# Output stores on ScalarE's queue, spread q loads and fewer w_out transfers in a fused linear-attention and mish kernel

## The chip, the cores and the metric

The kernel runs on one core of one Trainium2 chip. The time is device microseconds from one execution to its end, the median of three runs. PE is the matmul engine, PEld its weight loads, DVE VectorE, ACT ScalarE, POOL GpSimd; SP only issues transfers. DMA engines move data between HBM and the on-chip memory, and a transfer is issued by an instruction on the queue of SP or ACT.

## The reference

```python
kv  = einsum('bhsd,bhse->bhde', k, v)          # 8 x 8 heads, 576 tokens, 64 wide
out = einsum('bhsd,bhde->bhse', q, kv)
out = out / sqrt(mean(out * out, -1) + 1e-6) * g_norm
x   = out.transpose(0, 2, 1, 3).reshape(4608, 512)
h   = x @ w_in                                 # 512 x 2048
g   = h * tanh(softplus(h))                    # mish
return g @ w_out                               # 2048 x 512
```

All in float32; w_in and w_out arrive as float64 and are read as pairs of 32-bit words.

## The kernel before, in words

The work has two parts. The first computes x and g = mish(x @ w_in) and writes g to scratch memory in HBM (`gd`, nine tiles of 512 tokens); the second reads g back and multiplies by w_out.

Both products are done by a Winograd form of Strassen's scheme: seven products of half-size blocks instead of eight. Left forms (A11, S1, ...) come from the activations, right forms (B11, T1, ...) from the weights. Each form is split by `split` (L118 to L120) into a rounded part (an ACT cast) and a rest (a DVE subtraction), and each product takes three matmuls per slice.

Part one has nine blocks i of 512 tokens, each with four groups n (`NQ`), each group with seven steps, one for each product: 252 steps in all. A step is one of p0 to p6 in `group`. PE multiplies into two PSUM tiles `a` and two `bc`; ACT copies out of them (L372 to `ul`, L377 and L386 to `ur`), DVE adds (L427), ACT applies mish (L116), and the two finished tiles `ul` and `ur`, 512 KB each, are stored to `gd` (L425, L432). There are two rooms each for `ul` and `ur`: the copy of two groups later must wait for the store.

Beside the products of block i the attention of block i + 1 goes on: `kv_load` (L204, L205) and `kv_product` (L240) for k and v, a unit of two pairs of heads at a time for q (`load` L272, DVE transpose L285, projection L297 to L302, square L306, sums L317 to L320, Ln and Exp L325 and L326, normalize L330), and the left forms of the next x. ACT loads another function table when it changes between mish and Ln or Exp (L116, L324). Also beside it, w_out is read (L134, sixteen tiles of four source pieces), scaled and joined from its words (L139 to L146), made into forms (`wst`) and stored to scratch memory `wod` (L191). In the last block the forms of w_out come back (L550) into the rooms of w_in's forms, and g begins to be read (L555).

The order: `at(t, f)` puts a piece of work at step t of the plan, and the instructions are written in the plan's order. The compiler's scheduler orders PE, DVE, ACT and GpSimd itself; SP's queue stays as written (`manual_schedule` for SP), so SP issues each transfer only after those written ahead of it. All transfers, of either queue, share eight semaphores in turn, and a transfer waits for the last one on its semaphore to land.

Of the kernel before, what the change touches and what calls it, by code (L numbers as in the profile page):

```python
# [7 lines left out]
F32 = mybir.dt.float32  # L8
# [12 lines left out]

A11, S1, S2, S4, A12, S3, A22 = range(7)

T1, T3, T2, T4, B11, B22, B21 = range(7)

PROD = ((A11, B11, "a"), (S1, T1, "c"), (A22, T4, "p"), (S2, T2, "a"), (S4, B22, "c"), (A12, B21, "b"), (S3, T3, "a"))

# [2 lines left out]
def linear_attention_rms_mish_ffn(  # L30
# [95 lines left out]
    def weight_forms(srcs, m, n, forms, put=None):  # L126

        st = {}
        w = m * n

        def load():
            t = wpools["w64"].tile([P, 4, w, 2], U32, name="w64")
            for i, src in enumerate(srcs):
                nc.sync.dma_start(t[:, i].rearrange("p (m n) t -> p m (n t)", m=m), src)  # L134
            st["w"] = t.rearrange("p b n t -> p (b n) t")

        def scale():
            st["x"] = wpools["wx"].tile([P, 4 * w], F32, name="wx")
            nc.scalar.mul(st["x"], st["w"][:, :, 1].bitcast(F32), 2.0 ** -112)  # L139

        def join():
            low, high = st["w"][:, :, 0], st["w"][:, :, 1]
            t = st["x"].bitcast(U32)
            nc.vector.tensor_single_scalar(t, t, 3, ALU.logical_shift_left)
            nc.vector.scalar_tensor_tensor(t, high, 0x80000000, t, ALU.bitwise_and, ALU.bitwise_or)
            nc.vector.scalar_tensor_tensor(t, low, 29, t, ALU.logical_shift_right, ALU.bitwise_or)  # L146

        def differences():
            x = st["x"].rearrange("p (b n) -> p b n", b=4)
            d = st["w"].rearrange("p n t -> p (n t)").bitcast(F32)[:, 0:4 * w].rearrange("p (b n) -> p b n", b=4)  # L150
            nc.vector.tensor_sub(d[:, 0:2], x[:, 1:3], x[:, 0:2])
            nc.vector.tensor_sub(d[:, 2], x[:, 2], d[:, 0])
            nc.vector.tensor_sub(d[:, 3], x[:, 3], d[:, 2])
            st["x"], st["d"] = x, d
            st["f"] = forms()

        def parts(f0, f1, src):
            hi, lo = (st["f"][:, f0:f1, s].rearrange("p f m n -> p f (m n)") for s in range(2))
            split(hi, lo, src)

        def first():
            parts(T1, T4 + 1, st["d"])

        def rest():
            parts(B11, B11 + 1, st["x"][:, 0:1])
            parts(B22, B21 + 1, st["x"][:, 2:4])

        def store():
            put(st["f"])

        return load, scale, join, differences, first, rest, store
# [3 lines left out]
    def weight_in(j):  # L175
        def forms():
            wf[j] = wfp.tile([P, 7, 2, 2, P], F32R, name="wf")
            return wf[j]
        srcs = []
        for kh, r in ((0, 0), (0, 1), (1, 1), (1, 0)):  # L180
            c0 = 2 * P * (j + r * NF2)
            src = w_in[kh * 2 * P:(kh + 1) * 2 * P, c0:c0 + 2 * P]
            srcs.append(src.rearrange("(m p) n -> p m n", p=P))
        return weight_forms(srcs, 2, P, forms)

    def weight_out(c, h):
        def forms():
            return wpools["wst"].tile([P, 7, 2, 1, P], F32R, name="wst")

        def store(f):  # L190
            nc.sync.dma_start(wod[c][:, :, :, h * P:(h + 1) * P], f.rearrange("p f s m n -> p f s (m n)").bitcast(F32))  # L191
        srcs = []
# [27 lines left out]
    def kv_new(b):  # L220
        def new(name, dtype):
            t = kvs.tile([P, NKC, P], dtype, name=name)
            nc.vector.memset(t.bitcast(F32), 0.0)
# [28 lines left out]
    def segments(j):  # L252

        n = (S - T) * j
        segs = []
        if n:
            segs.append((j - 1, S - n, slice(0, n)))
        if n < T:
            segs.append((j, 0, slice(n, T)))
        return segs  # L260

    def unit_steps(j, u):
        st = {}

        def load(n):
            if n == 0:
                st["q"] = att.tile([P, 2, T], F32, name="qs")
            for i in range(2 * n % 4, 2 * n % 4 + 2):
                a, h, d0 = n // 2, 4 * u + 2 * (n // 2) + i // 2, 32 * (i % 2)
                for b, s0, cols in segments(j):  # L270
                    n_ = cols.stop - cols.start
                    nc.sync.dma_start(  # L272
                        st["q"][32 * i:32 * i + 32, a, cols].rearrange("p (c d) -> p c d", d=32),
                        q[b, h, s0:s0 + n_, d0:d0 + 32].rearrange("(c p) d -> p c d", p=32),
                    )

        def parts(t):
            hi = att.tile([P, 2, T], F32R, name="fh")
# [142 lines left out]
    def put_in(st, block, bank):  # L421
        o, i, n, t = u_dst(st, block), st["i"], st["n"], 7 * (NQ * st["i"] + st["n"])
        if block == "21":
            mish(o, bank)
            at(t + 11, lambda: nc.sync.dma_start(gd[i][:, 2 * n:2 * n + 2, :], st["ul"]))  # L425
            return
        nc.vector.tensor_add(o, bank, o)  # L427
        if block == "11":
            mish(o, o)
        elif block == "22":  # L430
            mish(st["ur"], st["ur"])
            at(t + 9, lambda: nc.sync.dma_start(gd[i][:, NF2 + 2 * n:NF2 + 2 * n + 2, :], st["ur"]))  # L432


    NS = 7 * NQ
# [8 lines left out]
    nc.vector.memset(eps, 1e-6)  # L444
    nc.vector.memset(ones.bitcast(F32), 0.0)
    nc.vector.memset(ones[0:D, 0:D].bitcast(F32), 1.0)
    nc.vector.memset(ones[D:P, D:P].bitcast(F32), 1.0)
# [5 lines left out]
    for step in START.split():  # L453
        what, n = step[0], int(step[1:])
        load, transpose, project, square, sums, rstd, normalize = units[0][n % 2]
        if what == "w":
            conv[n] = weight_in(n)
            conv[n][0]()
        elif what == "c":
            for f in conv[n][1:6]:  # L460
                f()
        elif what == "k":
            ts = []
            for m in range(2):
                ts.append(rooms[2 * n + m])
                ts.append(x[0:SL, 2 * n + m, 0:4 * D].rearrange("p (h d) -> p h d", h=4))
            kv_tiles[n] = kv_load(0, 4 * n, 4, ts)
        elif what == "m":
            kv_product(0, 4 * n, 4, *kv_tiles[n])
        elif what == "q":  # L470
            for i in range(4):
                load(i)
        elif what == "t":
            transpose()
            project()
        elif what == "s":
            square()
            sums()
        elif what == "r":
            rstd()  # L480
            normalize()
        elif what == "a":
            x_sums(n)
        elif what == "f":
            x_form(n)
# [10 lines left out]
    def attention(j):  # L496

        t = NS * (j - 1)
        if j < B:
            st = {}  # L500

            def kload(p):
                st[p] = kv_load(j, 2 * p, 2, kv_staging())

            def kmul(p):
                kv_product(j, 2 * p, 2, *st[p])
            at(t, lambda: kv_new(j))
            for p in range(4):
                at(t + 3 * p - 2 if p else max(t - 18, -1), lambda p=p: kload(p))
                at(t + 3 * p, lambda p=p: kmul(p))  # L510
        for u, ns in enumerate(((3, 5, 6, 8, 9, 10), (12, 14, 15, 17, 18, 19))):
            for s, n in enumerate(ns):
                at(t + n, units[j][u][s + 1])
            for n in range(4):
                at(t + 4 + n if u else max(t - 14 + n, -1), lambda u=u, n=n: units[j][u][0](n))
        at(t + 20, lambda: x_sums(0))
        for f, n in zip(range(7), (21, 22, 24, 25, 26, 27, 30)):
            at(t + n, lambda f=f: x_form(f))
            if f == S1:
                at(t + n, lambda: x_sums(1))  # L520
# [228 lines left out]
```

## Time and profile before

| | |
|---|---|
| time, median of three runs | 927.61 us (926.47 to 931.49) |
| profiled execution | 924.8 us, its span 923.0 us |
| mean granted clock of PE | 0.974 |
| busy: PE, DVE, ACT, POOL | 841.3, 597.7, 512.5, 0.2 us |
| moved by DMA | 160.50 MB, 174 GB/s over the span |

A busy PE is not a PE at its peak. Issues of transfers, register and semaphore instructions are not counted as busy. In the chain that ended last, "SPq" is time in SP's queue, "DMA" a transfer in flight, "issue" time without a cause in the profile. A line such as "PE a L409 <- ACT ul L116: 13.2, 5, 3.9" says who waited (engine, tile, line), for whom, how many us in all, how often, and the longest.

### The profile page before, as it was taken

The page shows a single profiled execution, that of the slowest core. Times are in us where ns is not written, and L with a number is a line of the kernel's source. Part 1 is how long each engine was busy: PE and PEld are TensorE (multiplying, and loading weights), DVE is VectorE, ACT ScalarE, POOL GpSimd, SP SyncE. Part 2 cuts the span into 40 slices and gives each one's busy share as a digit, 9 for nine tenths or more (in the row PEclk, how much of TensorE's full clock was granted, in tenths as well). Part 3 has the DMA queues.
Part 4 walks back from the last instruction along what each step waited for, and adds up shares of the span by engine and source line. Part 5 has one row for each costly group of instructions (what it writes and reads, how often), then busy time and mean ns, then how long its engine had stood idle before and what let it go on. Part 6 is the DMA issues. An engine that isn't in the chain of part 4 may idle for free.

```text
span 923.0 us, 17036 instructions
## 1 busy us (share of the span) xinstructions
PE 841.3 (91%) x6940; PEld 809.6 (88%) x6940; DVE 597.7 (65%) x842; ACT 512.5 (56%) x776; POOL 0.2 (0%) x4
## 2 busy tenths in 40 slices
PE   3498799897989889989899998999999999999997
PEld 1286699797988879989898998899999999999997
DVE  4688874836557465575755526867776677776661
ACT  2577666776567676677776534444444444444441
POOL 0000000000000000000000000000000000000000
PEclk9789899999999999999999999999999999999999
DMA  8557547766674776667463999433334433333411
GB/s 188 164 143 228 173 116 208 239 171 190 172 206 158 206 218 190 183 202 205 156 191 118 348 391 353 163 119 133 114 120 162 153 115 124 128 116 124 161 59 46
DMA packets 204973, 160.50 MB, mean 174 GB/s; under 512 B 91744, under 2 KB 190048, under 8 KB 203872
## 3 DMA queue, kind: packets, MB, share of 16 engines
q1 hardware_dynamic: 204896, 159.42, 56.1%
q8 instruction: 54, 0.88, 0.4%
q14 instruction: 23, 0.19, 0.1%
HBM read 97.52 MB, written 61.87 MB: 173 GB/s over the span
## 4 chain that ended last, share of the span: by engine, by line
PE 61%; SPq 13%; DMA 11%; ACT 10%; DVE 3%; issue 2%; ACTq 0%; DVEq 0%
PE a L598 21%; PE bc L598 16%; PE a L409 12%; SPq L272 8%; PE bc L409 7%; DMA wf<-wod 3%; SPq L134 3%; DMA gd<-ur 2%; DMA gd<-ul 1%; PE s L240 1%; PE q L666 1%; DMA w<-in_moe_w_out_dram 1%; ACT ur L116 1%; DMA w<-in_moe_w_in_dram 1%; ACT ul L116 1%
## 5 line engine op out<-in xcount | busy, mean ns | idle before, releaser
L409 PE MATMUL a<-gf,wf 128*128 128x256 f32 x1728 | 242.9, 293 | 34.0 <-ACT ul L116 13.2
L409 PEld LDWEIGHTS a<-gf,wf 128*128 128x128 f32 x1728 | 225.8, 198 | 43.5 <-ACT ul L116 14.3
L598 PE MATMUL a<-wf,gf 128*128 128x256 f32 x1632 | 203.4, 284 | 2.8 <-ACT ul L372 2.3
L598 PEld LDWEIGHTS a<-wf,gf 128*128 128x128 f32 x1632 | 199.6, 190 | 3.2 <-ACT ul L372 2.5
L409 PE MATMUL bc<-gf,wf 128*128 128x256 f32 x1296 | 180.2, 288 | 5.7 <-DVE wf L120 3.0
L409 PEld LDWEIGHTS bc<-gf,wf 128*128 128x128 f32 x1296 | 167.6, 195 | 8.8 <-DVE wf L120 3.5
L598 PE MATMUL bc<-wf,gf 128*128 128x256 f32 x1224 | 153.1, 284 | 0.2 <-DVE gf L120 0.2
L120 DVE TENSOR_TENSOR gf<-g,gf 128x1024 fp32r<-128x1024 f32 (+1 forms) x100 | 109.7, 1103 | 63.0 <-ACT gf L119 63.0
L598 PEld LDWEIGHTS bc<-wf,gf 128*128 128x128 f32 x1224 | 149.7, 189 | 0.4 <-DVE gf L120 0.4
L119 ACT CAST gf<-g 128x1024 fp32r<-128x1024 f32 (+1 forms) x100 | 94.5, 954 | 59.5 <-PE bc L598 55.2
L119 ACT CAST gf<-s 128x1024 fp32r<-128x1024 f32 (+2 forms) x58 | 49.2, 850 | 36.1 <-PE a L598 29.3
L120 DVE TENSOR_TENSOR gf<-s,gf 128x1024 fp32r<-128x1024 f32 (+2 forms) x58 | 56.3, 972 | 12.1 <-ACT gf L119 12.0
L372 ACT COPY ul<-a 128x512 f32<-128x512 f32 (+1 forms) x53 | 27.3, 516 | 47.6 <-PE a L598 29.3
L120 DVE TENSOR_TENSOR fl<-fa,fh 128x1024 fp32r<-128x1024 f32 x28 | 34.2, 1221 | 19.8 <-ACT fh L119 19.6
L427 DVE TENSOR_TENSOR ul<-bc,ul 128x512 f32<-128x512 f32 x36 | 24.8, 689 | 33.6 <-ACT ul L372 27.7
L116 ACT ACTIVATE ur<-ur 128x1024 f32<-128x1024 f32 x36 | 38.0, 1055 | 15.4 <-DVE ur L427 15.2
L427 DVE TENSOR_TENSOR ur<-bc,ur 128x512 f32<-128x512 f32 x36 | 24.8, 689 | 28.7 <-ACT ur L386 12.4
L120 DVE TENSOR_TENSOR gf<-gf 128x512 fp32r<-128x512 f32 x45 | 30.4, 685 | 13.6 <-ACT gf L119 12.0
L427 DVE TENSOR_TENSOR ur<-a,ur 128x512 f32<-128x512 f32 x36 | 24.7, 687 | 15.7 <-PE a L409 15.6
L116 ACT ACTIVATE ul<-a 128x512 f32<-128x512 f32 x36 | 21.4, 594 | 22.2 <-PE a L409 22.0
L330 DVE SCALAR_TENSOR_TENSOR gf<-x,gcol,fa 128x1024 f32<-128x1024 f32 x18 | 23.1, 1282 | 16.4 <-ACT fa L326 16.3
L139 ACT ACTIVATE wx<-w 128x512 f32<-128x512 f32 (+1 forms) x24 | 20.0, 833 | 23.4 <-DMA w<-in_moe_w_out_dram 13.3
(95 smaller groups left out, 843.0 us busy)
## 6 DMA issues: line engine op xcount, KB each, us to landing
g<-gd SPq DMA_DIRECT2D x18, 2048.0 KB, 8.7
gd<-ur SPq DMA_DIRECT2D x36, 512.0 KB, 3.1
gd<-ul SPq DMA_DIRECT2D x36, 512.0 KB, 3.8
wod<-wst SPq DMA_DIRECT2D x16, 896.0 KB, 5.3
wf<-wod SPq DMA_DIRECT2D x8, 1792.0 KB, 13.5
out_dram<-ul SPq DMA_DIRECT2D x18, 512.0 KB, 2.8
w<-in_moe_w_in_dram SPq DMA_DIRECT2D x32, 256.0 KB, 3.9
w<-in_moe_w_out_dram SPq DMA_DIRECT2D x64, 128.0 KB, 3.1
```

What stands on the lines that cost most here:

```text
L116: in_turn(nc.scalar.activation(o, i, AF.Mish))
L119: nc.scalar.copy(hi, src)
L120: nc.vector.tensor_sub(lo, src, hi.bitcast(F32))
L134: nc.sync.dma_start(t[:, i].rearrange("p (m n) t -> p m (n t)", m=m), src)
L139: nc.scalar.mul(st["x"], st["w"][:, :, 1].bitcast(F32), 2.0 ** -112)
L240: nc.tensor.matmul(ps[o * D:(o + 1) * D, i, :], kt, vt, start=(c == 0), stop=(c == CM))
L272: nc.sync.dma_start(st["q"][32 * i:32 * i + 32, a, cols].rearrange("p (c d) -> p c d", d=32), q[b, h, s0:s0 + n_, d0:d0 + 32].rearrange("( ...
L330: nc.vector.scalar_tensor_tensor(o, st["x"], gcol, st["r"], ALU.mult, ALU.mult)
L372: nc.scalar.copy(dst(st, "11"), st["a"])
L409: nc.tensor.matmul(bank[:, jj], w[:, right, a, kc, :], xf[:, b, kc, :], start=first and jj == kc == s == 0, stop=(kc == 1 and s == 2), ski ...
L427: nc.vector.tensor_add(o, bank, o)
L598: nc.tensor.matmul(bank, gf[:, a, c, :], wo[c][:, right, b, :], start=first and c == s == 0, stop=(c == NF2 - 1 and s == 2), skip_group_ch ...
```

## The change

Stores of `ul` and `ur` are issued by ACT, planned at t + 10 and t + 7 instead of t + 11 and t + 9. q is loaded in eight pieces of one 32-row part each instead of four of two parts, at steps t - 15, t - 13, ..., t - 1 for the first unit (before: t - 14 to t - 11) and t + 4 to t + 11 for the second (before: t + 4 to t + 7); its transposes stay at t + 3 and t + 12. A w_out tile is read by two transfers of 256 KB instead of four of 128 KB; for that the forms B22 and B21 change places. Ten memsets move from DVE to GpSimd.

```diff
-T1, T3, T2, T4, B11, B22, B21 = range(7)
+T1, T3, T2, T4, B11, B21, B22 = range(7)
...
         def load():
             t = wpools["w64"].tile([P, 4, w, 2], U32, name="w64")
+            n_ = 4 // len(srcs)
             for i, src in enumerate(srcs):
-                nc.sync.dma_start(t[:, i].rearrange("p (m n) t -> p m (n t)", m=m), src)
+                dst = t[:, i].rearrange("p (m n) t -> p m (n t)", m=m) if n_ == 1 else t[:, n_ * i:n_ * i + n_].rearrange("p b n t -> p b (n t)")
+                nc.sync.dma_start(dst, src)
...
-            nc.vector.tensor_sub(d[:, 0:2], x[:, 1:3], x[:, 0:2])
-            nc.vector.tensor_sub(d[:, 2], x[:, 2], d[:, 0])
-            nc.vector.tensor_sub(d[:, 3], x[:, 3], d[:, 2])
+            nc.vector.tensor_sub(d[:, 0:2], x[:, 1:4:2], x[:, 0:2])
+            nc.vector.tensor_sub(d[:, 2], x[:, 3], d[:, 0])
+            nc.vector.tensor_sub(d[:, 3], x[:, 2], d[:, 2])
...
-        for fh, r in ((0, 0), (0, 1), (1, 1), (1, 0)):
-            f0, c0 = (c + fh * NF2) * P, 2 * (r * DM // 2 + h * P)
-            srcs.append(w_out[f0:f0 + P, c0:c0 + 2 * P].rearrange("p (m n) -> p m n", m=1))
+        for fh in range(2):
+            f0 = (c + fh * NF2) * P
+            srcs.append(w_out[f0:f0 + P, :].rearrange("p (r h n) -> p r h n", r=2, h=2)[:, :, h, :])
...
-            nc.vector.memset(t.bitcast(F32), 0.0)
+            nc.gpsimd.memset(t.bitcast(F32), 0.0)
...
-            for i in range(2 * n % 4, 2 * n % 4 + 2):
-                a, h, d0 = n // 2, 4 * u + 2 * (n // 2) + i // 2, 32 * (i % 2)
+            a, i = divmod(n, 4)
+            h, d0 = 4 * u + 2 * a + i // 2, 32 * (i % 2)
...
-            at(t + 11, lambda: nc.sync.dma_start(gd[i][:, 2 * n:2 * n + 2, :], st["ul"]))
+            at(t + 10, lambda: nc.scalar.dma_start(gd[i][:, 2 * n:2 * n + 2, :], st["ul"]))
...
-            at(t + 9, lambda: nc.sync.dma_start(gd[i][:, NF2 + 2 * n:NF2 + 2 * n + 2, :], st["ur"]))
+            at(t + 7, lambda: nc.scalar.dma_start(gd[i][:, NF2 + 2 * n:NF2 + 2 * n + 2, :], st["ur"]))
...
-            for n in range(4):
-                at(t + 4 + n if u else max(t - 14 + n, -1), lambda u=u, n=n: units[j][u][0](n))
+            for n in range(8):
+                at(t + 4 + n if u else max(t - 15 + 2 * n, n // 2 - 1), lambda u=u, n=n: units[j][u][0](n))
```

SP's queue in the third block of part one (i = 2, `gd_92`), from the w_out words of one tile to those of the next, before:

```order
L134 DMA w_2068<-in_moe_w_out_dram 128x256 x4
L272 DMA qs<-in_q_dram 32x8x32 x4
L191 DMA wod_100<-wst 1792x1x128
L272 DMA qs<-in_q_dram 32x8x32 x8
L432 DMA gd_92<-ur 128x1024
L272 DMA qs<-in_q_dram 32x8x32 x4
L425 DMA gd_92<-ul 128x1024
L432 DMA gd_92<-ur 128x1024
L134 DMA w_2318<-in_moe_w_out_dram 128x256 x4
L425 DMA gd_92<-ul 128x1024
```

The same place in the changed kernel:

```order
L136 DMA w_2060<-in_moe_w_out_dram 128x2x256 x2
L274 DMA qs<-in_q_dram 32x8x32 x2
L193 DMA wod_100<-wst 1792x1x128
L274 DMA qs<-in_q_dram 32x8x32 x10
L136 DMA w_2304<-in_moe_w_out_dram 128x2x256 x2
L274 DMA qs<-in_q_dram 32x8x32 x2
L193 DMA wod_101<-wst 1792x1x128
L274 DMA qs<-in_q_dram 32x8x32 x2
```

The four stores are gone from SP's queue, and four of the sixteen pieces of q stand behind the next w_out words.

ACT's queue around the mish of the second `ur` of that block, before (its store is the first L432 above):

```order
L116 ACT_TABLE_LOAD
L116 ACTIVATE ul<-ul 128x2x256
L248 CAST kvh_350<-s_1978 64x64
L116 ACTIVATE ur<-ur 128x1024
L377 COPY ur<-bc 128x2x256
L119 CAST fh<-fa 128x1024
L248 CAST kvh_350<-s_1978 64x64
L116 ACTIVATE ul<-a 128x2x256
```

In the changed kernel, with the semaphores that each instruction waits for (DMAHW with a number is one of the eight of the transfers):

```order
L116 ACT_TABLE_LOAD
L116 ACTIVATE ul<-ul 128x2x256 [waits DVE_49]
L116 ACTIVATE ur<-ur 128x1024 [waits DVE_49]
L374 COPY ul<-a 128x2x256 [waits DMAHW0_49,PE_49]
L434 DMA gd_92<-ur 128x1024 [waits DMAHW5_49,Activation_49]
L250 CAST kvh_338<-s_1965 64x64 [waits PE_49]
L379 COPY ur<-bc 128x2x256 [waits DMAHW2_49,PE_49]
L250 CAST kvh_338<-s_1965 64x64 [waits DVE_49]
L116 ACTIVATE ul<-a 128x2x256 [waits PE_49]
L326 ACT_TABLE_LOAD
L427 DMA gd_92<-ul 128x1024 [waits DMAHW2_49,Activation_49]
```

Two stores now stand in ACT's order, each one or two instructions behind its mish; besides that mish each waits for a semaphore on which an earlier transfer, here of q on SP's queue, must have landed, and the copy of the next `ur` stands behind the first of them.

More of the change, by code (lines that the diff above doesn't have):

```diff
@@ L165, in rest @@
             parts(B11, B11 + 1, st["x"][:, 0:1])
-            parts(B22, B21 + 1, st["x"][:, 2:4])
+            parts(B21, B22 + 1, st["x"][:, 2:4])
         def store():
@@ L179, in weight_in @@
         srcs = []
-        for kh, r in ((0, 0), (0, 1), (1, 1), (1, 0)):
+        for kh, r in ((0, 0), (0, 1), (1, 0), (1, 1)):
             c0 = 2 * P * (j + r * NF2)
@@ L267, in load @@
                 st["q"] = att.tile([P, 2, T], F32, name="qs")
-            for i in range(2 * n % 4, 2 * n % 4 + 2):
-                a, h, d0 = n // 2, 4 * u + 2 * (n // 2) + i // 2, 32 * (i % 2)
[L270 to L275, printed above, removed]
+            a, i = divmod(n, 4)
+            h, d0 = 4 * u + 2 * a + i // 2, 32 * (i % 2)
+            for b, s0, cols in segments(j):
+                n_ = cols.stop - cols.start
+                nc.sync.dma_start(
+                    st["q"][32 * i:32 * i + 32, a, cols].rearrange("p (c d) -> p c d", d=32),
+                    q[b, h, s0:s0 + n_, d0:d0 + 32].rearrange("(c p) d -> p c d", p=32),
+                )
         def parts(t):
@@ L443, in linear_attention_rms_mish_ffn @@
         nc.sync.dma_start(gcol[r, :], g_norm.rearrange("(p o) -> p o", o=1))
[L444 to L447, printed above, removed]
+    nc.gpsimd.memset(eps, 1e-6)
+    nc.gpsimd.memset(ones.bitcast(F32), 0.0)
+    nc.gpsimd.memset(ones[0:D, 0:D].bitcast(F32), 1.0)
+    nc.gpsimd.memset(ones[D:P, D:P].bitcast(F32), 1.0)
     weight_pools(2, 1, 0)
@@ L470, in linear_attention_rms_mish_ffn @@
         elif what == "q":
-            for i in range(4):
+            for i in range(8):
                 load(i)
```

## The prediction, as it was on record before the run

> **What bounds the kernel now.** I read the page's busy line and its chain that ended last first, then a table of stretches, then the waits inside the stretch that has room, and last one event of the chain in order of time.
>
> ```profile
> PE 841.3 (91%) x6940; PEld 809.6 (88%) x6940; DVE 597.7 (65%) x842; ACT 512.5 (56%) x776; POOL 0.2 (0%) x4
> PE 61%; SPq 13%; DMA 11%; ACT 10%; DVE 3%; issue 2%; ACTq 0%; DVEq 0%
> ```
>
> PE looks full, yet 13% of the chain is SP's queue issuing transfers and 11% is transfers in flight. The stretches (start:end, length, then busy time of PE, weight loads, DVE, ACT, POOL, granted clock, DMA share, GB/s) say where that can be:
>
> ```profile
> 49.00:108.00 59.00, 47.86 (x370) 41.39 (x368) 51.29 (x78) 42.86 (x71) 0.00 (x0) 0.93 0.70 200
> 108.00:508.00 400.00, 368.60 (x3108) 353.48 (x3108) 246.06 (x420) 279.27 (x436) 0.00 (x0) 0.97 0.63 182
> 508.00:579.00 71.00, 65.41 (x533) 63.99 (x531) 36.31 (x74) 32.09 (x63) 0.00 (x0) 1.00 1.00 365
> 579.00:923.00 344.00, 338.95 (x2808) 338.54 (x2808) 235.13 (x231) 137.33 (x182) 0.00 (x0) 0.99 0.36 121
> ```
>
> From 579 us on PE is never short of work (339 of 344 us); the change does not reach there. From 508 to 579 the DMA engines are full (share 1.00) and PE has 5.6 us idle. The room is in the 400 us before: 31.4 us in which PE is idle. What ended that idle time (waiter, its line, released by: total us, times, longest):
>
> ```profile
> PE a L409 <- ACT ul L116: 13.2, 5, 3.9
> PE a L409 <- ACT ul L372: 9.0, 6, 3.8
> PE a L409 <- ACT ur L386: 5.1, 5, 1.9
> PE bc L409 <- ACT ur L377: 2.8, 3, 1.5
> ACT ul L372 <- DMA gd<-ul: 7.3, 7, 2.4
> ACT ur L377 <- DMA gd<-ur: 11.3, 7, 2.9
> ACT wx L139 <- DMA w<-in_moe_w_out_dram: 13.3, 10, 3.7
> SPq L432 <- ACT ur L116: 62.1, 13, 9.7
> SPq L204 <- PE s L240: 36.7, 11, 7.3
> ```
>
> 13.2 + 9.0 + 5.1 + 2.8 = 30.1 us of PE's idle time ends on ACT. ACT is no full engine (279 of 400 us): it waits 18.6 us for stores of earlier outputs, whose room it wants to write, and 13.3 us for words of w_out. Those transfers are late because SP issues everything in one written order: it stands 62.1 us before stores of ur whose mish is not done, and the loads behind stand with it; and a store that is ready stands behind the loads ahead of it. One event of the chain (start, us, what):
>
> ```profile
> 200.85 1.06 ACT ur L116
> ...
> 208.40 1.29 SPq L272
> ...
> 214.32 5.20 DMA gd<-ur
> 219.55 0.59 ACT ur L377
> 220.13 0.96 ACT fa L326
> 221.11 1.28 ACT L116
> 222.41 0.63 ACT ul L116
> 223.03 0.94 ACT ur L116
> 223.98 0.49 ACT ul L116
> 224.52 4.50 PE a L409 x24
> ...
> 358.43 2.92 PE a L409 x24
> 453.76 4.63 PE a L409 x24
> ```
>
> The mish of ur ends at 201.9; its store is issued at 214.3, 12.4 us late, behind eight pieces of q. It lands at 219.5, and only then ACT may copy into that ur again; behind it in ACT's order stand the Exp, a table load and three mishes, and PE waits for the last of them. After such a gap 24 matmuls take 4.50 or 4.63 us instead of 2.92: these two rows make 1.6 + 1.7 = 3.3 us more that belong to the gaps. PE's own timeline of the event, with the idle time before a piece in brackets:
>
> ```profile
> 220.18 1.69 PE L409 MATMUL bc<-gf,wf 128*128 128x256 f32 x12 [1.48 <-ACT ur L377]
> 224.52 4.49 PE L409 MATMUL a<-gf,wf 128*128 128x256 f32 x24 [2.65 <-ACT ul L116]
> ```
>
> **The change part by part.** Prices of an issue and of a landing:
>
> ```profile
> L425 SPq DMA_DIRECT2D gd<-ul x36: 319/389/1698, 84.6 to 562.1; - x36
> L432 SPq DMA_DIRECT2D gd<-ur x36: 319/350/2242, 81.0 to 561.4; - x36
> L272 SPq DMA_DIRECT2D qs<-in_q_dram x256: 311/467/2124, 6.7 to 470.9; - x128
> ...
> DMA to landing us min/median/max: 1.7/2.4/6.7
> ...
> L134 SPq DMA_DIRECT2D w<-in_moe_w_out_dram x64: 423/432/1823, 103.3 to 464.4; - x64
> gd<-ur SPq DMA_DIRECT2D x36, 512.0 KB, 3.1
> gd<-ul SPq DMA_DIRECT2D x36, 512.0 KB, 3.8
> w<-in_moe_w_in_dram SPq DMA_DIRECT2D x32, 256.0 KB, 3.9
> w<-in_moe_w_out_dram SPq DMA_DIRECT2D x64, 128.0 KB, 3.1
> ```
>
> Stores, the gain. Issued by ACT soon after its own mish, a store of ur lands some 3.1 us later and one of ul 3.8 us later, where their rooms are wanted about a group of seven steps later. A group takes (562.1 - 84.6)/35 = 13.6 us by the ul row, so the 18.6 us of ACT's waits for stores should go. SP loses 72 issues and the 62.1 us of standing still, so the w_out words come earlier too: I take half of 13.3, 6.6 us. In the event above ACT's wait is the longest of its kind, 2.9 us, and PE's two gaps behind it are 1.48 + 2.65 = 4.1 us: 2.9/4.1 is 70%. I take 70% of the 30.1 us: **-21.1 us**. Ends: all of it with the slow matmuls, -33.4, or nothing, if what is next in line is just as late (below). What is late next is ACT's own bunch of Exp, table load and mishes, 4.3 us in the rows above.
>
> Stores, the cost. The issue now stands in ACT's own order. No trace here shows an issue by ACT; the nearest rows are SP's issues of the same transfers, median 0.39 and 0.35 us, so 0.37 each (ends: the 0.32 of the smallest and the 2.2 of the longest, which came in the stretch with full DMA engines). 400/13.6 = 29.4 groups make 59 stores in the stretch with room, 59 x 0.37 = 21.8 us. Each waits for the mish that ACT itself has just done, so no other compute engine is waited for. Behind a store stand copies out of PSUM, and PE waits for those. ACT has 10% of the chain, 92 us, nearly all of it before 579 us, which is 16% there; with SP's and DMA's parts gone I let it double, to a third: 21.8 / 3 = **+7.3 us**. Ends: 0 and 21.8.
>
> The Trainium skill (DMA: Bandwidth & Descriptors, Issuing engines are not separate DMA queues) says that transfers issued by different engines run on the same 16 DMA engines and interleave, so that spreading them saves only the issuing engine's time, usually little. By that rule the term above would be +7.3 and the gain nearly none; against it stands the event above, where the loss was 12.4 us of standing in line and not bandwidth, at a DMA share of 0.63.
>
> q in eight pieces: the same 256 issues of 0.47 us. They are spread over fifteen and eight steps instead of four, and for the second unit the last piece stands one step (1.95 us) before its transpose instead of five, with an issue of two parts and a landing ahead of it, 2 x 0.47 and 2.4 us: 1.4 us late, eight times, and more at the longest landing, 6.7; but the steps only set SP's order, SP has nothing to wait for there after its k and v loads, and DVE, which transposes, is busy 246 of 400 us. PE has no wait on the projections in the stretch. I take 0; ends 0 and +10.
>
> w_out by two transfers: 32 fewer issues of 0.43 us, 13.8 us of SP's time, which no longer bounds. Landing: four issues and 3.1 us were 4.8; two issues and the 3.9 of a 256 KB load are 4.8. 0, ends -2 and +2. The order of the blocks inside the forms (B21 before B22) moves no work: one tensor operation reads with a step; 0.
>
> Memsets on GpSimd:
>
> ```profile
> L223 DVE MEMSET kvh<- x3: 485/485/485, 1.1 to 86.0; 128x512 f32 x3
> ```
> ```profile
> 32.34 0.26 ACT kvh L244
> ```
>
> DVE loses ten instructions, six of them of 0.49 us (three of kvh, as many of kvl). Four of the six come from 1.1 us on, before there are data; the last two, at 86 us, stand where DVE is busy 51 of 59 us, so up to -1. GpSimd's price isn't in the trace (its four memsets of one column are 0.2 us together); in the chain the first of these tiles is written by ACT at 32.3 us, so 30 us of loading cover it. 0; ends -1 and +2.
>
> The end of the first part. From 508 us two stores (1 MB, at 365 GB/s 2.9 us) of the last group no longer stand behind the last w_out forms in one queue but run beside them: +1.5, half of it; ends 0 and 2.9.
>
> Sum against the profiled execution's 924.8 us: -21.1 + 7.3 + 1.5 = -12.3, 912.5 us. That execution lies 2.8 below the median of the runs, 927.6; so **915 us**.
>
> **The rivals.**
>
> The bunch on ACT keeps its time. Exp, table load and the three mishes follow each other in any case, so a store that lands in time moves a gap without closing it. For it: 13.2 of the 30.1 us end on a mish and not on a copy. Against it: in the event the wait comes first. With 35% instead of 70%: -10.5 + 7.3 + 1.5 = -1.7, 926 us. The rule of the Trainium skill cited above, that only issue time is saved, would end here too.
>
> SP's queue leaves the chain altogether, and the matmuls after gaps run at full rate. 90% of 33.4 is -30.1; with a sixth of the issues on the path (+3.6) and the +1.5, -25.0: 903 us. For it: SPq is 13% of the chain, 120 us, far more than PE's idle time. Against it: ACT is at 70% and takes 21.8 us more.
>
> Slower: ACT inherits SP's wait. The order of instructions shows that a store on ACT waits for one of eight DMA semaphores that both queues share, so for an earlier load on SP, mostly a piece of q, to land; and SP still stands before its k and v loads until PE has used the last ones, 36.7 us in 11 waits. If ACT stands there with it, all of PSUM's copies stand behind: 0.7 x 36.7 = +25.7, so -12.3 + 25.7 = +13.4, 938 + 2.8 = 941 us. It decides from about 12.3/0.7 = 18 us of such waits on. Against it: the loads in question stand a few places ahead of the store, and SP no longer stands before stores.
>
> **How the numbers follow.** Chances: forecast (906 to 922) 0.59; SP gone from the chain (below 906) 0.10; bunch (923 to 932) 0.17; ACT inherits the wait (above 932) 0.14. The range reaches from the second rival's 903, less 3 for the lower ends of w_out and the memsets, to the edge of the slower case: 900 to 932. About 0.5%, 4.6 us, is what a measurement of this kernel can tell from no change: faster 0.69, same 0.17, slower 0.14.
>
> **What would show it.** Right: ACT's waits for gd in the first 508 us fall from 18.6 to under 5, for w_out words to under 8; stores are issued within 2 us of their mish; SPq falls from 13% of the chain to under 7; PE's idle time that ends on ACT falls to 8 to 15 us; ACT's queue issues 72 transfers of about 0.37 us; GpSimd has ten memsets more and no one waits for them. Wrong: ACT standing before its stores for pieces of q, or PE idle behind Exp and mishes as long as before (then the bunch bounds), or DVE's transposes waiting for the last piece of q and PE for the projections.

## The result and the profile after

The changed kernel is slower: 963.89 us, median of four runs (962.0 to 965.83), against 929.0 us (926.47 to 931.49). The ratio is 1.0376 with an interval of 1.0335 to 1.0417. The prediction said 915 us and 900 to 932. The profiled execution took 965.35 us, its span is 963.6 us and its mean granted clock 0.946 (before 0.974).

The busy line and the chain that ended last, of the page after:

```profile
PE 858.5 (89%) x6940; PEld 823.7 (85%) x6940; DVE 596.3 (62%) x832; ACT 510.3 (53%) x776; POOL 3.6 (0%) x14
PE 44%; DMA 6%; ACT 2%; DVE 1%; issue 1%; SPq 0%; ACTq 0%
```

DVE and ACT are busy no longer than before (ACT's 72 issues are not counted) and POOL has only the ten memsets more; PE's 6940 matmuls, the same as before, now take 17 us longer. The chain adds up to only 54% of the span, since it was not followed back through most of part one. That SPq stands at 0% in it therefore says nothing about the first part. The stretches say where the time is (columns as before):

```profile
49.00:108.00 59.00, 47.87 (x356) 41.91 (x355) 46.48 (x70) 40.08 (x67) 1.06 (x2) 0.86 0.68 183
108.00:544.00 436.00, 384.14 (x3138) 365.51 (x3138) 251.44 (x427) 280.35 (x443) 0.00 (x0) 0.93 0.59 172
544.00:620.00 76.00, 66.03 (x512) 64.67 (x511) 37.42 (x74) 32.28 (x62) 0.00 (x0) 0.94 0.88 336
620.00:963.00 343.00, 338.82 (x2804) 338.42 (x2803) 233.18 (x228) 135.51 (x178) 0.00 (x0) 0.99 0.36 119
```

The last 343 us are those of before. The loss lies ahead of them. Cut at the last matmul of part one, this is the first part before, then after:

```profile
49.00:560.40 511.40, 467.42 (x3896) 445.22 (x3894) 322.01 (x553) 347.41 (x560) 0.00 (x0) 0.97 0.67 203
```
```profile
49.00:598.50 549.50, 482.38 (x3886) 457.25 (x3886) 320.95 (x551) 344.19 (x560) 1.06 (x2) 0.93 0.62 189
```

It is 549.5 - 511.4 = 38.1 us longer. PE's idle time grew from 511.4 - 467.4 = 44.0 us to 549.5 - 482.4 = 67.1, by 23.1. The other 15.0 us are the same matmuls run at a granted clock of 0.93 instead of 0.97. What ended PE's idle time in the 436 us stretch:

```profile
PE a L411 <- ACT ul L116: 18.0, 8, 6.5
PE s L321 <- DVE fl L120: 9.7, 3, 6.0
PE a L411 <- DVE ur L429: 7.3, 4, 3.6
PE a L411 <- ACT ul L374: 4.5, 3, 2.7
PE a L411 <- ACT ur L388: 3.8, 3, 1.4
PE a L411 <- DVE wf L120: 3.2, 1, 3.2
PE bc L411 <- ACT ur L379: 3.0, 2, 2.7
```

The four rows of ACT that the prediction summed to 30.1 us now sum to 18.0 + 4.5 + 3.8 + 3.0 = 29.3: nothing was gained there. New are 9.7 + 7.3 + 3.2 = 20.2 us that end on DVE. What ACT and SP stood for in the same stretch:

```profile
ACT wx L141 <- DMA w<-in_moe_w_out_dram: 29.9, 11, 4.7
ACT fh L119 <- DVE fa L287: 16.6, 5, 5.5
ACT ul L374 <- DMA gd<-ul: 16.2, 11, 3.5
ACT wst L119 <- DMA wod<-wst: 11.1, 7, 3.4
```
```profile
SPq L206 <- PE s L242: 113.5, 18, 16.3
SPq L557 <- DVE gf L332: 21.0, 1, 21.0
SPq L274 <- DMA qs<-in_q_dram: 16.7, 8, 3.5
SPq L274 <- DVE fa L287: 16.1, 6, 9.0
```

ACT's wait for stores of `ur` (11.3 us before) has gone, but that for stores of `ul` has grown from 7.3 to 16.2 us, so of the 18.6 us for both, 16.2 are left. Its wait for words of w_out has grown from 13.3 to 29.9 us, and a wait for the transposes of q is new. SP no longer stands before stores: before, the two largest rows were 62.1 us there and 36.7 us before its k loads, 98.8 together, and now it is 113.5 us before the k loads alone. With the smaller rows of the same lines, SP stood 101.7 us before stores, 44.7 before k and v loads and 1.4 before pieces of q; now it is 128.4 us before k and v loads and 36.5 before pieces of q. The standing moved from one place of the queue to others, and the sum did not get smaller.

One event shows a path from there to PE. These are rows of the timeline of SP, ACT, DVE and PE (start, us, idle time before in brackets):

```profile
146.07 0.38 SPq L206 DMA_DIRECT2D km<-in_k_dram  x1
...
148.49 9.76 SPq L274 DMA_DIRECT2D qs<-in_q_dram  x6
158.29 1.24 SPq L136 DMA_DIRECT2D w<-in_moe_w_out_dram  x2
...
168.44 2.22 SPq L136 DMA_DIRECT2D w<-in_moe_w_out_dram  x2
...
155.19 1.25 DVE L287 STREAM_TRANSPOSE fa<-qs 128x1024 f32<-128x1024 f32 x1 [1.94 <-DMA qs<-in_q_dram]
...
156.48 1.05 ACT L119 CAST fh<-fa 128x1024 fp32r<-128x1024 f32 x1 [5.52 <-DVE fa L287]
162.48 0.67 ACT L141 ACTIVATE wx<-w 128x512 f32<-128x512 f32 x1 [3.46 <-DMA w<-in_moe_w_out_dram]
173.78 0.66 ACT L141 ACTIVATE wx<-w 128x512 f32<-128x512 f32 x1 [4.07 <-DMA w<-in_moe_w_out_dram]
...
178.81 5.49 PE L411 MATMUL a<-gf,wf 128*128 128x256 f32 x24 [6.47 <-ACT ul L116]
```

The k load at 146.07 is the first of the next block, planned at t + 10; SP reaches it when PE has done the product before it. The last of the second unit's eight pieces of q, two transfers, is planned behind it, at t + 11, and goes out from 148.49 on; before the change the last piece was planned at t + 7, ahead of this load. These two transfers took 5.3 and 6.3 us to land, where the median from 146 to 176 us is 2.3. The transpose, which needs all eight pieces, runs at 155.19 (in the profile before, the same one runs at 145.50), and ACT stands 5.5 us for it. There is one room for `qs`, so the next unit's pieces wait for this transpose, and the w_out words that are written behind them go out at 158.29. ACT stands 3.46 us for these words, and 4.07 us for those of the next tile, which go out from 168.44 on. The Exp, a table load and the mishes follow, and PE waits 6.47 us. What that gap costs on top is seen in the granted clock of the next 7 us (column before the last two):

```profile
178.81:186.00 7.19, 7.19 (x39) 7.19 (x40) 6.34 (x13) 6.89 (x15) 0.00 (x0) 0.61 0.74 292
```

At 0.61 of the full clock over these 7.19 us, and 0.50 while they ran (178.81 to 184.30), 24 matmuls took 5.49 us; the 24 that start at 149.43 took 3.04.

### The profile page after: what moved, and what is told of

Same layout as the page of the kernel before. It is cut to its first block, busy times and chain, and to the rows that moved or that the text cites. A ratio compares the mean times of both kernels' runs of the same rounds, so it can differ in the third digit from the quotient of the medians.

```text
span 963.6 us, 16994 instructions
## 1 busy us (share of the span) xinstructions
PE 858.5 (89%) x6940; PEld 823.7 (85%) x6940; DVE 596.3 (62%) x832; ACT 510.3 (53%) x776; POOL 3.6 (0%) x14
## 4 chain that ended last, share of the span: by engine, by line
PE 44%; DMA 6%; ACT 2%; DVE 1%; issue 1%; SPq 0%; ACTq 0%
PE a L600 20%; PE bc L600 15%; PE a L411 4%; PE bc L411 3%; DMA g<-gd 2%; DMA gd<-ul 2%; DMA wf<-wod 1%; PE q L668 1%; DMA vm<-in_v_dram 1%; DMA wod<-wst 1%; DVE gf L120 0%; DMA w<-in_moe_w_out_dram 0%; ACT L116 0%; ACT fa L328 0%; ACT ur L116 0%
## 5 line engine op out<-in xcount | busy, mean ns | idle before, releaser
L411 PE MATMUL a<-gf,wf 128*128 128x256 f32 x1728 | 254.8, 302 | 49.2 <-ACT ul L116 18.0
L411 PEld LDWEIGHTS a<-gf,wf 128*128 128x128 f32 x1728 | 236.4, 207 | 60.1 <-ACT ul L116 20.2
L411 PE MATMUL bc<-gf,wf 128*128 128x256 f32 x1296 | 183.3, 292 | 7.6 <-ACT ur L379 3.2
L411 PEld LDWEIGHTS bc<-gf,wf 128*128 128x128 f32 x1296 | 170.0, 198 | 11.4 <-ACT ur L379 4.7
L119 ACT CAST gf<-s 128x1024 fp32r<-128x1024 f32 (+2 forms) x58 | 49.1, 849 | 34.0 <-PE a L600 29.3
L374 ACT COPY ul<-a 128x512 f32<-128x512 f32 (+1 forms) x53 | 27.2, 516 | 60.2 <-PE a L600 29.3
L146 DVE TENSOR_SCALAR wx<-wx 128x512 uint32<-128x512 uint32 (+1 forms) x24 | 12.3, 513 | 51.3 <-ACT wx L141 51.3
L141 ACT ACTIVATE wx<-w 128x512 f32<-128x512 f32 (+1 forms) x24 | 19.8, 826 | 38.3 <-DMA w<-in_moe_w_out_dram 29.9
L119 ACT CAST fh<-fa 128x1024 fp32r<-128x1024 f32 x28 | 29.3, 1047 | 16.8 <-DVE fa L287 16.6
L120 DVE TENSOR_TENSOR gf<-gf 128x512 fp32r<-128x512 f32 x45 | 29.9, 682 | 8.9 <-ACT gf L119 8.9
```

The source lines that it names most:

```text
L119: nc.scalar.copy(hi, src)
L120: nc.vector.tensor_sub(lo, src, hi.bitcast(F32))
L374: nc.scalar.copy(dst(st, "11"), st["a"])
L411: nc.tensor.matmul(bank[:, jj], w[:, right, a, kc, :], xf[:, b, kc, :], start=first and jj == kc == s == 0, stop=(kc == 1 and s == 2), ski ...
```

## The experiments

Every kernel was timed beside the kernel before; "ratio" is to that, with its interval. The parts of the change, one at a time and in pairs, come first.

### Each part alone

`stores_alone`: the kernel before, with only this.

```diff
-at(t + 11, lambda: nc.sync.dma_start(gd[i][:, 2 * n:2 * n + 2, :], st["ul"]))
+at(t + 10, lambda: nc.scalar.dma_start(gd[i][:, 2 * n:2 * n + 2, :], st["ul"]))
-at(t + 9, lambda: nc.sync.dma_start(gd[i][:, NF2 + 2 * n:NF2 + 2 * n + 2, :], st["ur"]))
+at(t + 7, lambda: nc.scalar.dma_start(gd[i][:, NF2 + 2 * n:NF2 + 2 * n + 2, :], st["ur"]))
```

> The kernel before with the stores of ul and ur on ACT's queue (planned at t + 10 and t + 7) and nothing else. Theory A (the loss comes from the pieces of q that now stand ahead of the w_out words in SP's order): no loss here, 910 to 925 us, ACT's waits for w_out words at 13 us or less. Theory B (ACT's order carries the loss: issues, and copies behind stores): the larger part of the 35 us is here, 945 to 960 us. Theory C (the parts lose together only, since each new set of transfers gives the compiler another order): 920 to 940 us.

Measured: 927.29 us, ratio 0.999 (0.9963 to 1.0018). The part that was to bring 21 us brings nothing. Its waits from 108 to 508 us, of ACT, PE, and (to 544 us) SP:

```profile
ACT wx L139 <- DMA w<-in_moe_w_out_dram: 22.2, 7, 6.1
PE a L409 <- ACT ul L116: 15.6, 8, 4.5
...
ACT ul L372 <- DMA gd<-ul: 5.5, 4, 2.2
```
```profile
SPq L204 <- PE s L240: 83.1, 17, 15.3
```

The waits for stores fell from 18.6 to 5.5 us, near what was predicted, and those for w_out words rose from 13.3 to 22.2 instead of falling. SP stands 83.1 us before its k loads, where it was 36.7. So a longer stand there and longer waits for the words need not cost time.

`q_alone`: the kernel before, with q in eight spread pieces (the new `load` and its steps).

> The kernel before with q in eight spread pieces and nothing else. Theory A: the larger part of the loss is here, 945 to 960 us, ACT's waits for w_out words at 25 us or more. Theory B: no loss, 925 to 932 us. Theory C: 920 to 940 us.

Measured: 940.62 us, ratio 1.0143 (1.0085 to 1.0202). The term that the prediction set at 0 costs 13 us by itself. Its waits from 108 to 508 us, where the kernel before has neither row above 0.5 us:

```profile
PE x L300 <- ACT fh L119: 11.8, 6, 3.0
ACT fh L119 <- DVE fa L285: 11.0, 7, 4.3
```

PE's projections wait for ACT's cast, and the cast for the transpose. ACT's waits for w_out words, which theory A put at 25 us or more, fell to 6.4 us in this stretch, so the loss of this part does not come through the words.

`wout_alone`: two transfers a tile, and B21 and B22 changed over. `memsets_alone`: the ten memsets on GpSimd.

> The kernel before with two transfers for a w_out tile (and B21 before B22) and nothing else. Theories A and B: 920 to 930 us, since SP has 32 issues fewer and nothing else moves. Theory C: 920 to 940 us. If larger transfers land late in themselves: ACT's waits for w_out words above 20 us, and 935 us or more.

> The kernel before with its ten memsets on GpSimd and nothing else. Theories A and B: 925 to 932 us, no engine waits for GpSimd. Theory C: anything from 920 to 940 us, since the compiler's order after it may differ; what this run shows then is how far the time moves by order alone.

Measured: 920.64 us, ratio 0.9919 (0.9888 to 0.9951), and 925.6 us, ratio 0.9976 (0.9945 to 1.0008). The first is a gain of 7 us, the second not told from nothing. The four ratios add up to 0.28% over 1, some 3 us; the whole loses 3.76%. So the parts act on each other: of the three theories in these expectations, C, that the parts lose only together, has the most for it, though q alone lies just above its range, since q costs by itself. Nothing speaks for an ACT order that loses by itself.

### The change with one part undone

`after_q_as_before` and `after_stores_on_sp`: the changed kernel with the old `load` and its steps, and with the two stores back on SP at t + 11 and t + 9.

> The changed kernel with q loaded as before (four steps of two parts); stores on ACT, two w_out transfers and GpSimd memsets stay. The parts alone gave 0 (stores), +14 (q), -7 (w_out), -1 us (memsets), together +5, while the whole change gave +35. If q is a party to every loss (theory A): 917 to 925 us. If the stores on ACT and the other parts lose together without q (theory C): 935 us or more.

> The changed kernel with the stores back on SP's queue at t + 11 and t + 9; the rest of the change stays. If the parts add up: 931 to 937 us (q +14, w_out -7, memsets -1). If q in eight pieces loses more the less SP is held back by stores (the loss of q and the stores on ACT multiply): the same 931 to 937, and the 30 us that are missing in the sum belong to the pair. If q loses with w_out instead: 950 us or more.

Measured: 934.49 us, ratio 1.0069 (1.0045 to 1.0093), and 934.44 us, ratio 1.0059 (1.002 to 1.0098). Undoing either part takes most of the loss away. The first lies between the ranges of its two theories: without the spread of q, the stores on ACT still cost time beside the other two parts.

`after_q_second_unit_early` and `after_q_first_unit_early`: the changed kernel, with the spread undone for one of the two units.

```diff
-at(t + 4 + n if u else max(t - 15 + 2 * n, n // 2 - 1), ...)
+at(t + 4 + n // 2 if u else max(t - 15 + 2 * n, n // 2 - 1), ...)    # second unit early
+at(t + 4 + n if u else max(t - 14 + n // 2, -1), ...)                # first unit early
```

> The changed kernel, its q pieces of the second unit at the steps of before (t + 4 to t + 7, two a step), those of the first unit spread as changed. Theory A1: the last pieces of the second unit stand behind the k and v load that SP issues only when PE has used the last one, so the transpose comes late, the next unit's pieces wait for its room, and the w_out words behind them are late; then most of the loss goes, 918 to 935 us, and ACT's waits for transposes fall from 16.6 to under 5 us. Theory A2: the spread pieces of the first unit push the w_out words back by themselves: 950 us or more.

> The changed kernel, its q pieces of the first unit at the steps of before (t - 14 to t - 11, two a step), those of the second unit spread as changed. Theory A1: the loss stays, 950 us or more, with ACT's waits for transposes above 10 us. Theory A2: most of the loss goes, 918 to 935 us.

Measured: 939.34 us, ratio 1.0109 (1.0073 to 1.0144), and 951.31 us, ratio 1.0239 (1.0195 to 1.0283). The second unit's spread carries most: 24.6 of the 35 us come back without it, 12.6 without the first's. With the second unit early, 1.7 us of ACT's waits for transposes are left (before 545 us), of 16.6. That fits the event above, where the last of the second unit's pieces stands behind a k load; the time lies just outside theory A1's 918 to 935 us. What the first unit's spread does was not found.

### What does SP's standing cost, and through what?

The w_out words looked like the path from SP to ACT. Three kernels were to show it: the loads planned three steps earlier, in the changed kernel and with q as before, and the two harmless parts together without the others.

```diff
-        for s, n in enumerate((-8, 0, 1, 2, 3, 4, 6)):
+        for s, n in enumerate((-11, 0, 1, 2, 3, 4, 6)):
```

> The changed kernel with one edit: the loads of w_out words are planned three steps (5.9 us) earlier, at -11 instead of -8 from their tile's other steps. In the changed kernel ACT waits 29.9 us for these words before 545 us (longest 4.7) and 16.6 us for late transposes of q. Theory 1, both carry the loss (words late because SP stands, transposes late because the last pieces of q stand behind the k and v loads): the waits for words fall under 12 us, those for transposes stay over 12, the time is 948 us, 940 to 955. Theory 2, the late words carry all of it: under 940. Theory 3, the late transposes and ACT's own issues carry it and the words are only beside them: over 957 with the words' waits gone all the same.

> The changed kernel with q loaded in four pieces as before, and the loads of w_out words planned three steps earlier. With q as before alone it took 934.5 us, 16 more than the sum of the w_out and memset parts would give, and ACT waited 29.2 us for words of w_out. Theory 2, stores on ACT cost time because SP then stands before its k and v loads (100 us) with the w_out words behind them: those waits fall under 10 us and the time to 921 us, 917 to 926. Rival, the cost is ACT's own issues (some 60 of 0.33 us) and its changed order: over 930, whatever the words do.

> The kernel before with only two parts of the change: w_out words by two transfers and memsets on GpSimd; stores on SP and q in four pieces. If the parts add (-7.0 and -2.3 us measured one by one): 918.5 us, 915 to 921. If the memsets' part is nothing: 920.6. Above 924 if the gain of the two transfers came from an order of instructions that the memsets change.

Measured: 948.97 us, ratio 1.0205 (1.0157 to 1.0254); 933.9 us, ratio 1.0039 (1.0019 to 1.006); 919.59 us, ratio 0.9896 (0.986 to 0.9933). The third is the fastest kernel of the study: these two parts add, and they are the ones worth keeping. The first hit its number for a reason that was not the expected one, and the second missed: ACT waited 28.4 and 26.8 us for the words, as much as without the edit. The order of ACT's instructions shows why: the scale of the words was placed earlier along with the load, after 28, 40 and 53 of ACT's reads of `a` and `bc` for the third, fifth and seventh tile instead of 29, 43 and 56. Why the first gained 15 us all the same stays open. The steps of the plan set SP's order; the scale's place on ACT was the compiler's.

`after_transpose_later` moves the second unit's transpose, projection, square and sums to t + 14, 15, 16 and 17.

> The changed kernel with the second unit's transpose two steps (3.9 us) later, at t + 14, its projection, square and sums at t + 15, 16 and 17 (before 14, 15, 17), so that the last pieces of q have time to land. Theory 1: ACT's waits for late transposes (16.6 us, longest 5.5) fall under 5 us and the time by about 70% of that and of the 6 to 8 us that PE loses at full clock behind them, to 950 us, 943 to 957. Rival: the late pieces do their harm through the room of q and SP's queue, which a later transpose frees later still: 960 or more, with ACT's waits for w_out words at 30 us or above.

Measured: 962.09 us, ratio 1.0347 (1.0307 to 1.0387), with 15.3 us of ACT's waits for transposes: nothing moved. The instructions of DVE and ACT stand in the same order as in the changed kernel, row for row, so this was the changed kernel over again and told nothing about late transposes. It only confirms that the plan's steps do not place the work of these engines.

So the scales were held by force: an order without a semaphore, behind the last mish written ahead of them, in the changed kernel, with q as before, with the second unit's pieces early as well, and in the fastest kernel as a control.

```diff
-            nc.scalar.mul(st["x"], st["w"][:, :, 1].bitcast(F32), 2.0 ** -112)
+            i = nc.scalar.mul(st["x"], st["w"][:, :, 1].bitcast(F32), 2.0 ** -112)
+            if m == 1:
+                order = mybir.DependencyInfo(mybir.DependencyClass.NoSync, mybir.DependencyReason.DATA)
+                tc.add_manual_dep(i.ins, last[-1].ins.name, order, reason="words")
```

> The changed kernel with one edit: each scale of w_out words is held in ACT's order behind the last mish that the plan writes ahead of it (an order without a semaphore), which puts it 2 to 8 PSUM copies later than the compiler does by itself; loading the words earlier did not take ACT's waits for them away, because the compiler moved the scales earlier with them. Theory W, scales placed before their words have landed carry the part of the loss that appears with stores on ACT (16 us beside w_out and memsets): ACT's waits for words fall from 29.9 to under 8 us and the time from 964 to 945 us, 938 to 952; the late transposes stay, 13 to 20 us of waits. Rival R, the words' waits are only where ACT's slack shows, and the cost is the 0.33 us issues and the lost order: 957 or more with the words' waits gone.

> The changed kernel with q in four pieces as before and the scales held as in the run beside it. Theory W: ACT's waits for words fall from 29.2 to under 8 us, and the time from 934 to 920 us, 916 to 925, that of the w_out and memset parts without stores on ACT (919.6). Rival R: 930 or more.

> The changed kernel with both repairs: the scales held, and the second unit's eight pieces of q at t + 4 to t + 7, two a step (alone that took 939.3 us; the first unit stays spread, stores on ACT). If late words and late transposes are the whole loss: 922 us, 916 to 929. If a third cause is left in it, stores on ACT above all: over 932.

> The control: the kernel before with the w_out and memset parts only, stores on SP, and the same hold of the scales. Its ACT waited 16.0 us for words. If the hold by itself brings what lies in such waits: 915 us, 909 to 919; if the waits were slack: 918 to 922; above 924 if a late scale harms by itself (forms of w_out stored late).

Measured: 960.82 us, ratio 1.0344 (1.0287 to 1.0401); 941.74 us, ratio 1.0152 (1.0104 to 1.0199); 944.93 us, ratio 1.0178 (1.0112 to 1.0245); and the control 947.53 us, ratio 1.0217 (1.0169 to 1.0265). In all four ACT no longer waits for the words, and none is faster than without the hold by more than the intervals. The control lost 28 us. What is new in its SP queue (49 to 545 us):

```profile
SPq L196 <- DVE wst L120: 44.2, 5, 14.4
SPq L196 <- DVE wx L149: 15.5, 1, 15.5
```

A later scale makes the forms later, and SP now stands 59.7 us before their store, which is written ahead of other loads and, in the control, of the stores of `ul` and `ur`. This is the likely cause of the loss, and was not tested by itself. With the hold the stores on ACT are even the better choice, 941.7 against 947.5 us (four runs each, 940.5 to 942.7 and 947.2 to 948.8). So ACT's wait for the words is not, by itself, the price of the stores on ACT, and that price has no fixed sign.

### The same stores from a third queue

Last, the stores went to the queue of GpSimd, which is idle: with q as before and with q spread.

```diff
-nc.scalar.dma_start(gd[i]...
+nc.gpsimd.dma_start(gd[i]...
```

> The kernel with q in four pieces, two w_out transfers and memsets on GpSimd, its stores at the same steps but on the queue of GpSimd, which is idle. With them on SP this took 919.6 us, on ACT 934.5. Theory I, the price is the issues in ACT's own order (some 60 of 0.33 us before 545 us): without them the time is 918 us, 912 to 924, and SP stands before its k loads 90 us or more all the same. Theory O, the price comes from SP running ahead to its k loads, and from the order that the compiler gives ACT, DVE and PE for it, with scales that wait for words of w_out: 929 to 938, ACT's waits for words 20 us or more.

> The changed kernel with its stores on GpSimd's queue instead of ACT's, all else as in it. On ACT it took 963.9 us, with the stores on SP 934.4. Theory I: 934 us, 926 to 942. Theory O: 955 or more, with ACT's waits for words above 20 us and for late transposes above 11.

Measured: 930.26 us, ratio 1.0049 (1.002 to 1.0077), and 951.42 us, ratio 1.0283 (1.0235 to 1.0331). Of the second, ACT's and SP's waits (49 to 540 us):

```profile
ACT wx L141 <- DMA w<-in_moe_w_out_dram: 26.5, 12, 4.5
...
ACT fh L119 <- DVE fa L287: 14.5, 5, 5.5
```
```profile
SPq L206 <- PE s L242: 114.1, 21, 16.7
```

They look as with the stores on ACT, though ACT issues nothing. The first time lies in theory O's range, the second between the two theories, nearer to O. With the two w_out transfers and the memsets in all six kernels, the ratios to the kernel before make a table:

| | stores on SP | on GpSimd | on ACT |
|---|---|---|---|
| q in four pieces | 0.9896 | 1.0049 | 1.0069 |
| q in eight, spread | 1.0059 | 1.0283 | 1.0376 |

Beside the two w_out transfers and the memsets, taking the stores off SP costs 1.5% with q as before and 2.2% with q spread (14 and 21 us of 928). The issues in ACT's own order, against GpSimd's, cost 0.2% (the intervals overlap) and 0.9% (9 us; the intervals just clear each other). The spread of q costs 1.6, 2.3 and 3.1% from left to right. So most of the stores' price comes with their leaving SP (the freed queue, or the order that the compiler then gives the other engines) and not with ACT's work.

## Why the prediction was wrong

**Stores, the gain (-21.1).** The step that failed: "SP loses 72 issues and the 62.1 us of standing still, so the w_out words come earlier too." SP did lose them, and the stores went out at once (in the event's stretch a mish of `ur` ends at 147.33 us and its store is issued at 147.36; 0.03 us is also the median of the 72). But SP is paced by PE at its k loads, for which there is one room; freed at the stores it stood there for 113.5 us, and the words did not come earlier: ACT waited 29.9 us for them instead of the 6.6 that were to be left. Counted in steps of PE (12 matmuls of part one each), the words of the last fifteen tiles were issued on average 0.2 of a step later than before in `stores_alone` and 0.7 later in the changed kernel. The waits for stores, all of which were to go, fell only to 16.2 us in the changed kernel. The idle time of PE that ends on ACT stayed (29.3 against 30.1 us), so the 70% had nothing to work on. Alone this part measured nothing, beside two w_out transfers and the memsets a loss of 1.7%. The rule weighed in the prediction, of the Trainium skill (DMA: Bandwidth & Descriptors, Issuing engines are not separate DMA queues), that another issuing engine saves only issue time, was nearer for this part alone: 0.999. It has no place for the loss beside the other parts.

**Stores, the cost (+7.3).** Right in kind. The issues and the events that they wait for, on ACT's queue (ns, shortest, median, longest):

```profile
L434 ACTq DMA_DIRECT2D gd<-ur x36: 326/327/607, 64.5 to 597.3; - x36
L434 ACTq EVENT_SEMAPHORE  x27: 17/17/17, 64.1 to 537.7; - x27
```

An issue took 0.327 us where 0.37 was taken, and against GpSimd's queue the price was 2 us with q as before and 9 us with q spread. The slower rival had ACT standing before its stores for earlier loads on the shared semaphores. The second row alone does not settle this (before the scale at 173.78, for which ACT stood 4.07 us, the same instruction took under 0.04 us), but the start times do: none of the 72 stores was issued more than 0.13 us after the end of ACT's instruction ahead of it. So ACT never stood there. The side of that rival came true, and SP's stand before its k and v loads, which it also named, grew, but it did not reach ACT by these semaphores.

**q in eight pieces (0, ends 0 and +10).** The step that failed: "the steps only set SP's order, SP has nothing to wait for there after its k and v loads". The next block's first k load stands among the pieces once they reach to t + 11, so that the last of them can go out only when PE has done the product before that load. The prediction had even worked out that the last piece would be 1.4 us late for its transpose, and dropped the term because DVE is not full and PE showed no such wait before. It cost 13 us alone, beyond the end of its bound, and 2.3 to 3.1% beside stores that were not on SP.

**w_out by two transfers (0, ends -2 and +2).** Mis-sized: -7 us. PE's idle time on the four rows of ACT fell from 30.1 to 24.0 us in that kernel, but whether the fewer issues or the changed order of the forms did it was not taken apart. **Memsets (0):** right, 0.9976 with 1 in the interval.

**The clock.** The prediction let the slow matmuls behind gaps make 3.3 us on 30.1. In the changed kernel 15.0 us of slower matmuls came with 23.1 us more idle time. The longest wait on a mish is 6.5 us where it was 3.9, and the event shows the clock at 0.61 behind it. The Trainium skill (TensorE: Matmul & The Clock Gate, Part 1: The HAM clock gate) puts the drop to half rate behind an idle stretch of about 3.4 us; the 0.50 behind the gap of 6.47 us agrees with that. The event of the prediction does not: there 24 matmuls took 4.49 us at a clock of 0.64 behind gaps of 1.48 and 2.65 us, both shorter, so shorter gaps cost clock here too.

**The sum.** Terms were added as if each part met the kernel before. Measured alone they do sum to almost nothing (+0.3%). They do not add: beside the two w_out transfers and the memsets, the spread of q costs 1.6%, the stores on ACT 1.7% and both 4.8%, so some 1.4% (13 us) comes only with the pair. The event gives a reason, a queue that stands at a load with one room and pieces that were put behind that load, and the run with the second unit's pieces early bears it out: ACT's waits for transposes went from 16.6 to 1.7 us and 24.6 us came back.

**What stays open.** How the freed SP costs 14 us with q as before. The traces of all such kernels without the hold share two marks, 80 to 115 us before the k loads and 22 to 30 us of ACT's waits for the words. `stores_alone` has both marks too (83.1 and 22.2 us) and lost nothing, and taking the second away by a hold brought new waits in its place. Nor were the words late there: with q as before, stores on ACT and two w_out transfers they were issued at the same step of PE, on average, as with the stores on SP (0.05 of a step later). Slower landings are no better: the 256 KB of v landed in 3.3 us before, in 4.2 in the changed kernel and in 4.5 in `stores_alone`. No kernel with a second room for k and v was timed. The compiler also orders PE, DVE and ACT anew when the stores leave SP, and its part was not isolated.

## What to carry to other kernels

When an in-order queue is freed from a wait, look for the next instruction on it that waits for a busy engine: here it stood there instead, and what was written behind that place came no earlier; ask what that is before counting the old wait as a gain. Spread a load over more steps only if no piece falls behind an instruction that another engine holds up, and price the last piece, since the consumer needs them all. Where the parts of a change share a queue, time them in pairs: here four parts that sum to +0.3% made +3.8%, and the two good ones were worth -1.0%.

## What the hardware showed that was not expected

An issue of a 512 KB store took 0.327 us on ACT's queue, less than the 0.350 and 0.389 us on SP's, and 0.531 us on GpSimd's, in the row of `ur` of the kernel with the stores there:

```profile
L434 POOL DMA_DIRECT2D gd<-ur x36: 531/531/721, 66.1 to 584.3; - x36
```

The landing was no quicker from either: 4.1 us for `ur` and 4.9 us for `ul` from ACT, 3.8 and 4.9 from GpSimd, 3.1 and 3.8 from SP before. And the same matmuls took 15 us longer when the gaps before them grew from 44 to 67 us in all.
